# Sigmoid attention and gated FFN on one core: two loads ahead of the unit matrix, the first transposes in half banks, FFN chunk 0 one unit earlier

## The chip, the core and the metric

The kernel runs on one core of one Trainium2 chip. The time is device microseconds (us) of one execution, launch to end. Five engines work side by side, each in its own program order: TensorE (PE, matrix products and transposes; PEld is its loading of weights), VectorE (DVE), ScalarE (ACT), GpSimd (POOL) and SyncE (SP). Three of them issue DMA transfers: SP and ACT through hardware queues, POOL through a software queue that can also convert float32 to float16 on the way. PE writes its results to PSUM, eight banks of 2 KB in each of 128 partitions; DVE and ACT read them from there.

## The reference

Inputs `q`, `k` and `v` have 8 batches, 12 heads, 448 positions and 64 dimensions, in float32. For each batch and head

```python
scores = scale * np.matmul(q, k.transpose(0, 1, 3, 2)) - np.log(S)   # S = 448, scale = 1/8
attn   = 1.0 / (1.0 + np.exp(-scores))                               # sigmoid, no row sums
out    = np.matmul(attn, v)
```

The heads are then put side by side (3584 rows of 768), and a gated feed-forward layer follows, with `w_gate` and `w_val` of 768x1536 and `w_out` of 1536x768:

```python
gate = np.maximum(x @ w_gate, 0.0)
val  = x @ w_val
y    = gate * val @ w_out
```

## The kernel before

**Layout.** The 448 positions of a batch are seven chunks of 64. Six pairs of heads are handled in three groups (`NG = 3`) of four heads. Everything that PE multiplies is float16. Scores are built transposed (keys on the partitions), so that the sigmoid's output can go straight into the product with `v`.

**What has to happen first.** For a group, the keys and queries must be transposed on PE: a transpose is a matmul against a unit matrix (`ident`, built on POOL by `make_identity`, two instructions). `transposed(b, g, ti, c0, c1)` (L199) takes one PSUM bank, transposes chunks c0 to c1 of keys (ti 0) or queries (ti 1) into it, two matmuls a chunk, and returns a function that copies the bank to `qkT` on DVE (L212). `pe_transposes` calls both at once.

**The first loads.** The first four chunks of keys and queries of group 0 come as float32 through the queues of SP and ACT (L126) and are converted to float16, keys on DVE (L679) and queries on ACT (L680). All other loads come through POOL's queue (`load`, L110; `load_v`, L114 and L116; `load_gv`, L148) in the order in which they are written: the remaining keys of group 0, keys and queries of groups 1 and 2, the rest of the queries of group 0, `v`, then the gate and value weights in slices `load_gv(f0, f1)`. Before the first of them POOL builds the unit matrix.

**Batch 0.** Batch 0 is not done like the others, since PE and ACT have to start before much has been loaded. Six slots (`FirstSlot`, L271) run in order: groups 0, 1, 2 with query chunks 0 to 3 (slots 0 to 2), then groups 0, 1, 2 with query chunks 4 to 6 (slots 3 to 5). A slot has four units: unit u multiplies key chunks 2u and 2u+1 with the slot's queries (L240: eight matmuls, four in the last unit) into a pair of PSUM banks, and ACT takes the sigmoid of it (L188). There are two such pairs (`pairp`, `bufs=2`), handed out in turn. So unit n may write only when the sigmoid of unit n-2 has been taken.

**The order by hand.** Instructions stand as the program writes them (`manual_schedule`), no planner moves them. The dictionary `after` says what PE does behind unit u of slot i: transposes, `slots[j].pv` (the product with `v`, L258, and its copy to `xT` on DVE, L185), `ffn_mix(1)`, which takes the next FFN chunk off a queue (`gv`, L312: six gate and six value matmuls, L317, and DVE or ACT work), or `keep_warm` (L172), matmuls on zeros whose result nobody reads, called fillers below. The four other PSUM banks (`bank`) are handed out in turn to transposes, fillers, `pv` and FFN chunks. Around the change the order is: transposes of the second half of the queries behind unit (3, 2); chunk 0 behind (3, 3); chunk 1 and then `pv` of slot 3 behind (4, 1); chunk 2 behind (4, 3). An FFN chunk of the first half needs `pv` of slots 0, 1 and 2, and its two slices of the weights. Chunks 0 and 1 use the first slices, `load_gv(0, 2)`; chunk 2 the next, `load_gv(2, 4)`.

Batches 1 to 7 then follow with units of whole 448 queries, FFN work in between, and the products of the FFN by a scheme with fewer multiplications (L401); the change does not touch these.

Of the kernel before, what the change touches and what calls it, by code (L numbers as in the profile page):

```python
# [17 lines left out]
def kernel(  # L18
# [10 lines left out]
    nc = tc.nc  # L29

    B, H, S, D = q.shape
# [8 lines left out]
    QCUT = 4  # L40
# [35 lines left out]
    def bank(name, shape=(P, 512), dtype=FP32):  # L76
        pool, tag = free[0]
        free.rotate(-1)
        return pool.tile(list(shape), dtype, tag=tag, name=name)

    def bank16(name):
        return bank(name, (P, 1024), FP16)
# [11 lines left out]
    def tiles_of(b):  # L94
        if b not in in_tiles:
            pool = early if b == 1 else inp
            in_tiles[b] = tuple(
                p.tile([P, NPAIR, NCH * D], FP16, tag=t, name=t)
                for p, t in ((pool, "k16"), (pool, "q16"), (vinp, "v16"))
            )  # L100
        return in_tiles[b]

    def rows_of(src, b):
        return src[b].rearrange("(x r) (t c) d -> (r t) x (c d)", r=2, c=NCH)

    def load(b, g0, g1, which, c0=0, c1=NCH):
        for nm, t16, src in zip("kq", tiles_of(b), (k, q)):
            if nm in which:
                xs, cs = slice(2 * g0, 2 * g1), slice(c0 * D, c1 * D)
                nc.gpsimd.dma_start(t16[:, xs, cs], rows_of(src, b)[:, xs, cs])  # L110
# [10 lines left out]
    KCUT = 4  # L121
    first32 = []
# [4 lines left out]
        first32.append(t32)  # L127
    zeros = early.tile([P, S], FP16, name="zeros")
    nc.vector.memset(zeros[:], 0.0)
    ident = early.tile([P, P], FP16, name="ident")  # L130
    make_identity(nc, ident[:])
    load(0, 0, 1, "k", KCUT)
    gate = const.tile([P, 2], FP16, name="gate")
    for g in range(1, NG):
        load(0, g, g + 1, "k")
        load(0, g, g + 1, "q", 0, QCUT)
    load(0, 0, 1, "q", QCUT)
    load_v(0)
# [30 lines left out]
    xT_tiles = {}  # L169
    hT_tiles = {}  # L170

    def keep_warm(count, parts=1):  # L172
        ps = bank("warm_ps")
        n = S // parts
        for _ in range(count * parts):
            nc.tensor.matmul(ps[:, 0:n], zeros[:, 0:P], zeros[:, 0:n], start=True, stop=True)  # L176

    def put_xT(b, pr, q0, qn, src):
# [12 lines left out]
    def qkT_of(b, g):  # L191
        if (b, g) not in qkT_tiles:
            qkT_tiles[(b, g)] = qkTp.tile([P, TW, P], FP16, tag="qkT", name="qkT")
        return qkT_tiles[(b, g)]

    def pe_transposes(b, g, ti, c0=0, c1=NCH):
        transposed(b, g, ti, c0, c1)()

    def transposed(b, g, ti, c0, c1):  # L199
        t16 = in_tiles[b][ti]  # L200
        qkT = qkT_of(b, g)
        trt = bank16("trt")
        for c in range(c0, c1):
            for h in range(2):
                nc.tensor.transpose(  # L205
                    trt[64 * h : 64 * h + 64, c * P : (c + 1) * P],
                    t16[:, 2 * g + h, c * D : (c + 1) * D],
                    ident[:],
                )

        def copy(a0=c0, a1=c1):
            nc.vector.tensor_copy(  # L212
                qkT[:, ti * NCH + a0 : ti * NCH + a1, :].rearrange("p c x -> p (c x)"),
                trt[:, a0 * P : a1 * P],
            )

        return copy
# [449 lines left out]
    def ffn_mix(count, hooks=()):  # L667
        hooks = list(hooks)
        for left in range(count, -1, -1):
            while hooks and hooks[0][0] >= left:  # L670
                hooks.pop(0)[1]()
            if left:
                gv_queue.popleft()()


    nc.scalar.activation(gate[:], zeros[:, 0:2], AF.Sigmoid, bias=sig_bias, scale=qk_scale)
    keep_warm(10, 2)
    k16, q16, _ = in_tiles[0]
    nc.vector.tensor_copy(k16[:, 0:2, 0 : KCUT * D], first32[0])  # L679
    nc.scalar.copy(q16[:, 0:2, 0 : QCUT * D], first32[1])  # L680
    pe_transposes(0, 0, 0, 0, KCUT)
    pe_transposes(0, 0, 1, 0, QCUT)
    keep_warm(2, 2)
    slots = [FirstSlot(half * NG + g, g, half) for half in range(2) for g in range(NG)]
    push_first(0, range(0, 4), False)
    def second_queries():
        for g in range(1, NG):
            pe_transposes(0, g, 1, QCUT, NCH)

    def first_of_second_group():  # L690
        pe_transposes(0, 1, 0, 0, KCUT)
        pe_transposes(0, 1, 1, 0, QCUT)
# [8 lines left out]
        keys(0, 3)  # L701
        keys(3, NCH)

    def ffn_then_pv(i):
        ffn_mix(1)
        slots[i].pv()


    after = {
        (0, 0): lambda: pe_transposes(0, 0, 0, KCUT, NCH),  # L710
        (0, 1): lambda: keep_warm(2, 2),
        (0, 2): first_of_second_group,
        (0, 3): lambda: pe_transposes(0, 1, 0, KCUT, NCH),
        (1, 0): lambda: keep_warm(2, 2),
        (1, 1): lambda: pe_transposes(0, 2, 0),
        (1, 2): lambda: pe_transposes(0, 2, 1, 0, QCUT),
        (1, 3): lambda: keep_warm(2),
# [3 lines left out]
        (2, 3): slots[1].pv,  # L721
        (3, 1): slots[2].pv,
        (3, 2): second_queries,
        (3, 3): lambda: ffn_mix(1),
        (4, 1): lambda: ffn_then_pv(3),
        (4, 3): lambda: ffn_mix(1),
        (5, 1): lambda: pv_then_ffn(4),
        (5, 3): first_of_second_batch,
# [78 lines left out]
    for b in range(1, B):  # L807
# [10 lines left out]
        count = len(bursts)  # L818
# [115 lines left out]
```

## Time and profile before

| | |
|---|---|
| median of 3 runs | 392.06 us (391.92 to 392.45) |
| the profiled execution | 392.07 us |
| its span, first to last instruction | 390.3 us |
| PE busy | 384.5 us, 99% of the span |
| ACT busy | 228.0 us, 58% |
| DVE busy | 283.0 us, 73% |
| POOL busy | 50.8 us, 13% |
| first filler on PE starts | 1.16 us |
| first sigmoid on ACT starts | 7.05 us |

The 1.8 us between the span and the execution's time lie before the first and behind the last instruction. Times in the profile count from the span's start. A busy PE is not PE at its peak: matmuls overlap, and their ends are modelled. In the chain of waits each piece is the work, or the wait, that the next piece had to have; a change of time that does not show on this chain does not show in the total. In a timeline, consecutive instructions of one kind are merged into a line: start, length of the merged stretch, and how many they are.

### The profile page before, as it was taken

Reading aid. Unit: us, or ns where it says so; the run is one execution under the profiler, and the core shown is the slowest. Engines: PE = TensorE matmul, PEld = TensorE weight load, DVE = VectorE, ACT = ScalarE, POOL = GpSimd, SP = SyncE. Lnnn points to the kernel's source line nnn. Section 1 sums busy time; section 2 is a strip of 40 time slices with the busy share of each in tenths; the row PEclk is TensorE's granted clock in tenths of the full one; section 3 lists DMA queues with packets and bytes.
Section 4 is the critical chain, followed back from the end, with each engine's and each line's share of the span. In section 5 each row is a group of like instructions: output and inputs, shape, how many; then the busy total and the mean of one; then the engine's idle time right before and its main releaser. Section 6 shows DMA issues by size and latency. Waiting matters only on the chain.

```text
span 390.3 us, 8791 instructions
## 1 busy us (share of the span) xinstructions
PE 384.5 (99%) x3504; PEld 217.9 (56%) x3504; DVE 283.0 (73%) x557; ACT 228.0 (58%) x482; POOL 50.8 (13%) x75
## 2 busy tenths in 40 slices
PE   8999999999999999999999999999999999999995
PEld 6678776445455545454555554545455555555663
DVE  2453444367387789999758789999987788999563
ACT  4957886784877755555547774545467354333322
POOL 8643404300310300003000300000000000000000
PEclk9999999999999999999999999999999999999999
DMA  9999996997998990226946695132003220000335
GB/s 149 199 199 204 204 203 116 205 204 123 193 187 165 154 236 15 49 47 70 186 94 122 130 206 96 28 66 41 10 22 72 73 79 2 0 3 0 80 89 156
DMA packets 68985, 43.69 MB, mean 112 GB/s; under 512 B 35920, under 2 KB 65616, under 8 KB 68944
## 3 DMA queue, kind: packets, MB, share of 16 engines
q0 software_dynamic: 30768, 23.34, 39.6%
q1 hardware_dynamic: 37664, 19.24, 23.8%
q10 hardware_dynamic: 512, 0.56, 0.5%
q8 instruction: 27, 0.44, 0.4%
q14 instruction: 14, 0.11, 0.1%
HBM read 47.19 MB, written 11.01 MB: 149 GB/s over the span
## 4 chain that ended last, share of the span: by engine, by line
PE 95%; ACT 3%; DVE 1%; issue 0%; DVEq 0%; ACTq 0%
PE u L401 33%; PE g L401 16%; PE y L401 11%; PE qk_ps L240 9%; PE g_ps L317 8%; PE pv_ps L258 8%; PE v_ps L317 7%; ACT PT L188 3%; PE ya L362 1%; PE warm_ps L176 1%; PE trt L205 1%; PE yb L362 1%; DVE ysb L471 0%; DVE S L392 0%; DVE hT L392 0%
## 5 line engine op out<-in xcount | busy, mean ns | idle before, releaser
L188 ACT ACTIVATE PT<-qk_ps 128x448 f16<-128x448 f32 (+3 forms) x318 | 150.9, 585 | 75.2 <-PE qk_ps L240 74.9
L401 PEld LDWEIGHTS <-S 128*128 128x128 f16 x558 | 54.6, 98 | 44.7
L613 DVE TENSOR_TENSOR gsb<-g,gsb 128x448 f32<-128x448 f32 x72 | 42.9, 625 | 10.3 <-PE g L401 10.0
L240 PE MATMUL qk_ps<-qkT 64*64 64x448 f16 (+2 forms) x756 | 47.8, 336 | 0.6 <-ACT PT L188 0.3
L401 PEld LDWEIGHTS <-hT 128*128 128x128 f16 x306 | 28.7, 98 | 22.2 <-issue 4.8
L335 DVE TENSOR_TENSOR hT<-gate_sb,v_ps 128x256 f16<-128x256 f32 (+2 forms) x36 | 16.4, 465 | 33.5 <-PE v_ps L317 16.2
L609 ACT COPY gsb<-u 128x448 f32<-128x448 f32 x48 | 25.6, 558 | 24.0 <-PE u L401 22.9
L453 ACT ACTIVATE ysb<-u 128x384 f32<-128x384 f32 x31 | 15.2, 491 | 38.2 <-PE u L401 33.8
L258 PE MATMUL pv_ps<-PT,v 64*64 64x448 f16 (+2 forms) x756 | 36.9, 329 | 0.0
L185 DVE TENSOR_SCALAR xT<-pv_ps 128x448 f16<-128x448 f32 (+2 forms) x53 | 27.9, 566 | 11.1 <-PE pv_ps L258 10.0
L317 PE MATMUL g_ps<-xT,wg 128*128 128x256 f16 (+2 forms) x216 | 33.5, 291 | 0.0
L317 PE MATMUL v_ps<-xT,wv 128*128 128x256 f16 (+2 forms) x216 | 33.3, 290 | 0.0
L401 PEld LDWEIGHTS <-wg 128*128 128x128 f16 x216 | 20.2, 98 | 21.8 <-issue 4.3
L401 PEld LDWEIGHTS <-wv 128*128 128x128 f16 x216 | 21.1, 98 | 19.7
L240 PEld LDWEIGHTS <-qkT 64*64 64x64 f16 x756 | 18.3, 105 | 21.3 <-issue 14.8
L471 DVE SCALAR_TENSOR_TENSOR ysb<-y,ysb 128x384 f32<-128x384 f32 x29 | 16.1, 556 | 17.9 <-PE y L401 10.4
L258 PEld LDWEIGHTS <-v 64*64 64x64 f16 x756 | 22.0, 107 | 10.5 <-issue 0.7
L110 POOL DMA_DIRECT2D k<-in_k_dram x15 | 11.5, 770 | 109.5 <-DVE rel L223 104.2
L401 PE MATMUL u<-T,hT 128*128 128x384 f16 x132 | 25.1, 326 | 0.0
L317 PEld LDWEIGHTS <-wg 128*128 128x128 f16 x216 | 18.8, 98 | 10.7 <-issue 4.4
L317 PEld LDWEIGHTS <-wv 128*128 128x128 f16 x216 | 20.1, 98 | 7.5
L401 PE MATMUL u<-xT,wg 128*128 128x448 f16 x108 | 23.5, 354 | 0.0
(76 smaller groups left out, 535.5 us busy)
## 6 DMA issues: line engine op xcount, KB each, us to landing
out_dram<-ysb SPq DMA_DIRECT2D x52, 192.0 KB, 2.9
v<-in_v_dram POOLq DMA_DIRECT2D x8, 336.0 KB, 14.8
v<-in_v_dram POOLq DMA_DIRECT2D x16, 168.0 KB, 14.8
k<-in_k_dram POOLq DMA_DIRECT2D x4, 672.0 KB, 11.9
q<-in_q_dram POOLq DMA_DIRECT2D x4, 672.0 KB, 15.3
k<-in_k_dram POOLq DMA_DIRECT2D x9, 224.0 KB, 12.2
q<-in_q_dram POOLq DMA_DIRECT2D x7, 224.0 KB, 12.3
wo<-in_moe_w_out_dram POOLq DMA_DIRECT2D x1, 1536.0 KB, 11.9
```

Of the source, the lines that this page charges most:

```text
L110: nc.gpsimd.dma_start(t16[:, xs, cs], rows_of(src, b)[:, xs, cs])
L185: nc.vector.tensor_scalar(out=xT, in0=src, scalar1=XSCALE, scalar2=None, op0=AOP.mult)
L188: nc.scalar.activation(PT_ap, ps_ap, AF.Sigmoid, bias=sig_bias, scale=qk_scale)
L240: nc.tensor.matmul(out_of(hh)[o : o + 64, :], qkT[rows, c, cols], qkT[rows, NCH + c0 : NCH + c1, cols], start=True, stop=True, tile_positi ...
L258: nc.tensor.matmul(ps[hh][64 * r : 64 * r + 64, 0:qn], v16[rows, 2 * g + hh, c * D : (c + 1) * D], pieces[c][rows, hh, :], start=(c == 0), ...
L317: nc.tensor.matmul(ps[-1][:, 0:qn], wt[:, dc, f * P : (f + 1) * P], xT_tiles[b][:, dc, q0 : q0 + qn], start=(dc == 0), stop=(dc == NDC - 1),)
L335: nc.vector.tensor_tensor(out=hT_tiles[g][:, f, o : o + qn], in0=gate_sb[:, 0:qn], in1=ps[1][:, 0:qn], op=AOP.mult,)
L401: nc.tensor.matmul(ps[:, 0:n], A[:, k_, :], W[:, k_, :], start=(first and k_ == 0), stop=(k_ == kn - 1), skip_group_check=True,)
L453: nc.scalar.activation(o, ps[:, 0:HM], AF.Copy, scale=OUT_SCALE)
L471: nc.vector.scalar_tensor_tensor(out=o, in0=ps[:, 0:HM], scalar=OUT_SCALE, in1=o, op0=AOP.mult, op1=AOP.add)
L609: by(gs[u][i][:], ps[u][:, 0:S])
L613: nc.vector.tensor_tensor(out=gs[u][i][:], in0=ps[u][:, 0:S], in1=gs[u][i][:], op=AOP.add)
```

## The change

On POOL, two loads that stood behind the unit matrix now stand ahead of it: the last three key chunks of group 0 and all keys of group 1. The loads behind them stay in their order.

On PE, the 20 fillers of 224 columns at the start become 22 of 194, and the four fillers between the first transposes and the first unit become two. The first keys and queries (four chunks each) are transposed into four banks of two chunks instead of two banks of four chunks, and copied by four DVE copies of 256 columns instead of two of 512. The copy of key chunks 2 and 3 is the last of the four. The conversion of the first queries is divided: ACT has the first two chunks, DVE the other two. The four fillers behind units (0, 1) and (1, 0) are written in another way, but are the same four matmuls.

FFN chunk 0 moves from behind unit (3, 3) to ahead of it, right behind the transposes; chunk 1 moves from behind unit (4, 1) to ahead of it; `pv` of slot 3 stays behind (4, 1), and chunk 2 behind (4, 3).

```diff
+    load(0, 0, 1, "k", KCUT)
+    load(0, 1, 2, "k")
     ident = early.tile([P, P], FP16, name="ident")
     make_identity(nc, ident[:])
-    load(0, 0, 1, "k", KCUT)
     gate = const.tile([P, 2], FP16, name="gate")
     for g in range(1, NG):
-        load(0, g, g + 1, "k")
+        if g > 1:
+            load(0, g, g + 1, "k")
         load(0, g, g + 1, "q", 0, QCUT)
...
-    def keep_warm(count, parts=1):
+    def keep_warm(count, n=S):
         ps = bank("warm_ps")
-        n = S // parts
-        for _ in range(count * parts):
+        for _ in range(count):
             nc.tensor.matmul(ps[:, 0:n], zeros[:, 0:P], zeros[:, 0:n], start=True, stop=True)
...
-    keep_warm(10, 2)
+    keep_warm(22, 194)
     k16, q16, _ = in_tiles[0]
     nc.vector.tensor_copy(k16[:, 0:2, 0 : KCUT * D], first32[0])
-    nc.scalar.copy(q16[:, 0:2, 0 : QCUT * D], first32[1])
-    pe_transposes(0, 0, 0, 0, KCUT)
-    pe_transposes(0, 0, 1, 0, QCUT)
-    keep_warm(2, 2)
+    half = QCUT // 2 * D
+    nc.scalar.copy(q16[:, 0:2, 0:half], first32[1][:, :, 0:half])
+    nc.vector.tensor_copy(q16[:, 0:2, half : QCUT * D], first32[1][:, :, half:])
+    transposed(0, 0, 0, 0, 2)()
+    other_keys = transposed(0, 0, 0, 2, KCUT)
+    transposed(0, 0, 1, 0, 2)()
+    transposed(0, 0, 1, 2, QCUT)()
+    other_keys()
+    keep_warm(2, S // 2)
...
     def second_queries():
         for g in range(1, NG):
             pe_transposes(0, g, 1, QCUT, NCH)
+        ffn_mix(1)
...
-    def ffn_then_pv(i):
-        ffn_mix(1)
-        slots[i].pv()
...
         (3, 2): second_queries,
-        (3, 3): lambda: ffn_mix(1),
-        (4, 1): lambda: ffn_then_pv(3),
+        (4, 0): lambda: ffn_mix(1),
+        (4, 1): slots[3].pv,
         (4, 3): lambda: ffn_mix(1),
```

More of the change, by code (lines that the diff above doesn't have):

```diff
@@ L702, in first_of_second_batch @@
         keys(3, NCH)
-    def ffn_then_pv(i):
-        ffn_mix(1)
-        slots[i].pv()
     after = {
         (0, 0): lambda: pe_transposes(0, 0, 0, KCUT, NCH),
-        (0, 1): lambda: keep_warm(2, 2),
+        (0, 1): lambda: keep_warm(4, S // 2),
         (0, 2): first_of_second_group,
         (0, 3): lambda: pe_transposes(0, 1, 0, KCUT, NCH),
-        (1, 0): lambda: keep_warm(2, 2),
+        (1, 0): lambda: keep_warm(4, S // 2),
         (1, 1): lambda: pe_transposes(0, 2, 0),
```

## The prediction

> **What bounds the kernel now.** I read the page's busy shares first, then the chain of waits, then the timeline where the change is made.
>
> ```profile
> PE 384.5 (99%) x3504; PEld 217.9 (56%) x3504; DVE 283.0 (73%) x557; ACT 228.0 (58%) x482; POOL 50.8 (13%) x75
> ...
> PE 95%; ACT 3%; DVE 1%; issue 0%; DVEq 0%; ACTq 0%
> ```
>
> PE is the bound of the whole; ACT holds 3% of the chain. The chain of waits of the first 40 us shows where:
>
> ```profile
> 1.16 3.92 PE warm_ps L176 x20
> 5.08 0.99 PE trt L205 x15
> ...
> 7.05 3.35 ACT PT L188 x4
> ```
>
> So the first 7 us are a run-up (first keys, transposes, copies, first scores), 7.05 to 17.14 is bound by ACT, and from 17.18 on every piece is PE's. A microsecond saved before 7.05, or one lost by PE after 17.18, shows in full at the end. The run-up in the timeline:
>
> ```profile
> 4.42 0.43 DVE L679 CAST k<-ysb 128x512 f16<-128x512 f32 x1 [3.32 <-DMA ysb<-in_k_dram]
> 4.71 0.62 ACT L680 CAST q<-ysb 128x512 f16<-128x512 f32 x1 [1.94 <-DMA ysb<-in_q_dram]
> 5.01 0.64 PE L205 MATMUL trt<-ident,k 128*64 128x128 f16 x8
> 5.43 0.64 PE L205 MATMUL trt<-ident,q 128*64 128x128 f16 x8
> 5.69 0.85 DVE L212 COPY qkT<-trt 128x512 f16<-128x512 f16 x2 [0.84 <-PE trt L205]
> 6.00 0.56 PE L176 MATMUL warm_ps<-zeros 128*128 128x224 f16 x4
> ```
>
> The 20 fillers start 0.187 us apart (3.92 less the last one's 0.39, over 19), the four at 6.00 only 0.096 apart (0.56 less 0.26, over 3): PE's clock doubles in between. The transposes still go at the slow rate, two every 0.106 us (four such steps from 5.01 to 5.43), while those at 6.93 need 0.053. The trace's clock record has the full clock from 5.94. And the place of the moved chunks:
>
> ```profile
> 18.85 0.28 PE L240 MATMUL qk_ps<-qkT 64*64 64x192 f16 x4
> 19.06 0.83 PE L317 MATMUL g_ps<-xT,wg 128*128 128x256 f16 x6
> ...
> 20.47 0.53 PE L240 MATMUL qk_ps<-qkT 64*64 64x192 f16 x16
> 20.93 0.83 PE L317 MATMUL g_ps<-xT,wg 128*128 128x256 f16 x6
> 20.95 1.51 ACT L188 ACTIVATE PT<-qk_ps 128x768 f16<-128x768 f32 x2 [1.16 <-PE qk_ps L240]
> ...
> 22.34 0.77 PE L258 MATMUL pv_ps<-PT,v 64*64 64x192 f16 x28
> ```
>
> PE never stands here. ACT takes units (4, 0) and (4, 1) 0.48 us behind their start on PE, while PE works on chunk 1.
>
> **The change, part by part.** The sum is made against the profiled execution: 392.07 us, of which 390.3 are the span and 1.77 lie around it. It is within 0.01 of the median (392.06).
>
> *Fillers and the first transposes.* 22 fillers of 194 columns at the slow rate take 22 x 0.187 x 194/224 = 3.56 us for 3.73, so the last ends 0.17 earlier. Before, the transposes could start 0.32 us behind the last filler's start at 4.68, which is 5.00. Now they wait for the key conversion, 4.42 + 0.43 = 4.85, plus some 0.05 for the signal (the pause between a copy's end, 6.54, and the scores that wait for it, 6.59): 4.90. Gain 0.10.
>
> *Half banks.* Two copies of 512 columns in a row (0.85) become four of 256. Copies of 512 and 384 take 0.423 and 0.354 in the profile, so 256 take 0.285 by the same slope, an estimate. From 4.90 the transposes go through four banks, four matmuls (0.21) each: first keys 4.90, other keys 5.11, first queries 5.32, other queries 5.53. Each bank is ready 0.42 + 0.05 behind its start (0.106 to its last pair, that pair's 0.31, the signal). DVE copies the first keys at 5.37, the first queries at 5.79 to 6.07, the other queries at 6.07 to 6.36. The first unit needs these three only, so it starts at 6.41 for 6.59. The other keys' copy, 6.36 to 6.64, is needed by the transposes behind the unit, at 6.75. The halved conversions are hidden: on ACT 256 columns are some 0.41 (between 0.62 for 512 and 0.20 for the 2 columns of the gate), so 4.71 to 5.12, used at 5.32; DVE's half lies at 4.85 to 5.14, used at 5.53. If that cover went, each late 0.1 would be a late 0.1 of the first unit. Two fillers for four: they end near 6.1, ahead of 6.41, so this is worth nothing as long as the clock rises at 5.94; their removal is cover only for a late clock. Sum of the run-up: -0.19. ACT's stretch starts 0.19 earlier and PE follows it at 17.18.
>
> *The loads on POOL.* The two loads start at 0.74 instead of 1.44 (behind them the unit matrix ends near 3.0, used at 4.90); from the third load on, at 3.02, POOL's queue stands as before. SP and ACT issue nothing new. What it does to the first keys and queries no row shows directly. Bounds: in the DMA view from 1.80 to 3.69 us and then to 4.30
>
> ```profile
> q1 hardware_dynamic: 259, 0.26, 57.6%
> q10 hardware_dynamic: 173, 0.18, 26.3%
> ```
> ```profile
> q0 software_dynamic: 150, 0.06, 78.8%
> q10 hardware_dynamic: 99, 0.09, 40.6%
> ```
>
> POOL's queue (q0) moves nothing until 3.70, although its first load was issued at 1.44. Later in the trace, on an idle queue, a load issued at 63.87 has its first packet 1.46 us later and one at 220.43 after 2.19. So the first was due at 2.9 to 3.6, and waited until the hardware queues were done on each DMA engine. If it waits again, the cost is nothing. If it is served in turn instead from 3.0 on, when some 118 packets of keys and 230 of queries were still to come (7 and 14 on each of 16 engines, at 0.05 us a packet in between), keys land up to 0.38 and queries up to 0.71 later. Working the steps above through from there, the first unit starts at 6.84: +0.25 in place of -0.19. I take nothing, because that is what the row of this very moment shows, and keep +0.44 as the other end. The Trainium skill's page "DMA: Bandwidth & Descriptors", section "Queues, rings and completion order", says that a DMA engine serves its queues in turn, a whole packet of descriptors at a time. By it the sum would take the upper end; the trace, where q0 had nothing before 3.70, does not agree so far. The later landings can only move forward or stay; the closest one, the value weights of chunk 2, lands at 23.93, and PE starts on them at 23.97.
>
> *Chunk 0 and chunk 1.* No work is added; the order decides. Rows: a chunk with the change to scores behind it is 1.41 (19.06 to 20.47); score matmuls up to the next FFN chunk 0.21 for 4, 0.35 for 12, 0.46 for 16; 8 of them up to a `pv` 0.18; a `pv` up to the next scores 0.60. On the old clock, without the gain of the run-up: chunk 0 at 18.85 (its weights land at 16.1 and 19.15, used from 19.4), units (3, 3) and (4, 0) at 20.26, chunk 1 at 20.62, unit (4, 1) at 22.03, `pv` at 22.21, unit (4, 2) at 22.81 and (4, 3) at 22.98. That is 0.13 ahead of the 23.11 of before, since one change between scores and FFN has gone. But (4, 3) writes the pair of banks that ACT reads for (4, 1). ACT now starts on that at 22.03 + 0.48 = 22.51 and needs 0.81 (half of 1.51 and a little, its two overlap): 23.32, with the signal 23.37. Before, this sigmoid ended at 22.46 and nobody waited. Behind the waiting matmul on PE stands chunk 2, and all that follows. So PE loses 0.39 and has 0.13 back: +0.25. Between 0 (if ACT were not later) and +0.35.
>
> *Sum.* 392.07 - 0.19 + 0.25 = 392.13, forecast 392.1: no change that can be measured (0.2%, or 0.78 us, is about what a measurement of this kernel can tell).
>
> **The rivals.**
>
> *The new wait doesn't form, the rest holds.* For it: ACT's lag is read from a merged line. Against it: the same lag of 0.47 to 0.48 stands at (5, 0). Then -0.19 - 0.13: 391.75.
>
> *The early loads hold up the first keys and queries.* As above: 392.07 + 0.25 + 0.25 = 392.6.
>
> *The clock rises later (slower).* This is the one that ends on the other side. The full clock came at 5.94, 4.8 us behind the first filler. The change takes away 0.17 us of early fillers and two later ones, so PE stands more before 5.94. If that is too little work for the rise, PE goes on at half speed. A slot of four units holds, at the full clock, about 0.75 us of score matmuls (seven chunks at 0.107), 0.75 of transposes (14 pairs at 0.053), 0.4 of fillers (four at 0.096) and eight changes of shape at about 0.09: 2.6 of ACT's 3.35. At half speed that is near 4.8, so PE becomes the bound and loses some 0.4 us for every microsecond. Two more slow microseconds decide: 0.8. Up to 4.8 more (as long as it took the first time) give +1.9. The Trainium skill's page "TensorE: Matmul & The Clock Gate", Part 1, has a free-running window of 3413 ns that must be busy; one more window would be 3.4 us, so an estimate of +1.4 us. Against this rival: 3.56 us of unbroken fillers remain, and PE's stretch from 2.5 to 5.9 loses only some 0.2. I take the middle of the 0.8 and the 1.9, +1.35: 393.5.
>
> *Late clock in most runs of before (faster).* If the rise usually came behind 6.75, the four fillers cost 0.75 and the change saves 0.37 more; with no new wait, 392.07 - 0.32 - 0.37 = 391.4, and somewhat below if the transposes gain too. The runs lie between 391.92 and 392.45, which leaves little room for it.
>
> **How the numbers follow.** Forecast 0.45 (391.8 to 392.4), no new wait 0.19, held-up loads 0.16, late clock 0.14, late clock before 0.06. Faster by over 0.2% needs 391.3 or less: 0.06, the last case and its tail. Slower needs 392.85 or more: the late clock and a little of the held-up loads, 0.16. The rest is 0.78. The range runs from 391.4 to 392.9: the three middle cases with their bounds, leaving out the late clock and the lower tail.
>
> **What would show it.** First transposes at 4.90 and first unit near 6.4, first sigmoid near 6.86: run-up right. Conversion of the keys starting later than 4.45: loads held up. Filler spacing of 0.19 behind the transposes, or transposes at 0.106 behind unit (0, 0): late clock. An idle PE of about 0.4 us before the last four score matmuls of slot 4, released by ACT: the new wait. A total outside 391.4 to 392.9 means a mechanism that I did not see, or the late clock.

## The result and the profile after

The changed kernel takes 392.74 us (median of 22 runs, 392.12 to 394.02), the kernel before 392.17 (median of 22 runs beside it, 391.91 to 393.07). The ratio, which rests on all runs and not on the medians alone, is 1.0018, with an interval of 1.0011 to 1.0025. So the changed kernel is slower by some 0.18%: the interval excludes no change at all, but the loss is inside the 0.2% that I count as no change. The 22 runs fall into two groups with nothing between: twelve from 392.12 to 392.75 (their middle is 392.39) and ten from 393.39 to 394.02 (393.58). I call the second one the upper group; the kernel before has one run in 22 above 393.0. The median of 392.74 is thus the top edge of the lower group and stands for neither. The lower group lies 0.22 above the kernel before; the larger part of the loss is the upper group. Two executions of the kernel before, beside the last runs below, took 844.33 and 2242.19 us and are left out of all counts. The profiled execution of the changed kernel is the fastest of the lower group, 392.12 us with a span of 390.3, so its profile shows what becomes of the run-up's gain, but not the upper group.

The page's busy shares and the shares of the chain have hardly moved (PE had 384.5 us and 95% of the chain, and the chain had no DMA in it):

```profile
PE 383.9 (98%) x3504; PEld 217.8 (56%) x3504; DVE 283.2 (73%) x560; ACT 227.8 (58%) x482; POOL 50.7 (13%) x75
...
PE 93%; ACT 3%; DVE 1%; DMA 1%; issue 0%; ACTq 0%; DVEq 0%
```

The chain of waits of the changed kernel up to 24 us (start, length, what) shows both halves of the change:

```profile
0.74 3.73 DMA ysb<-in_k_dram
...
4.50 0.55 DVE k L680
...
5.10 0.32 PE trt L206 x4
...
5.44 0.72 DVE qkT L213 x3
...
6.21 0.44 PE qk_ps L241 x8
...
6.67 3.35 ACT PT L189 x4
...
18.54 0.76 PE g_ps L318 x6
19.30 0.78 PE v_ps L318 x6
...
21.87 0.32 PE qk_ps L241 x8
...
22.27 0.82 ACT PT L189
...
23.13 0.28 PE qk_ps L241 x4
23.41 0.76 PE g_ps L318 x6
```

The first scores start at 6.21 (before: 6.59) and the first sigmoid at 6.67 (before: 7.05), a lead of 0.38. Chunk 0 starts 0.6 earlier. But ACT is on the chain again at 22.27, where it was not before, and chunk 2 starts at 23.34 by the timeline, 0.04 later than before (23.30). From there on the two profiles run side by side, 0.02 to 0.04 apart. The timeline names both losses. Its columns are start, length, engine and line, what and how many, and in brackets the idle time ahead and what ended it. First the kernel before, where units (4, 2) and (4, 3) run in one stretch:

```profile
19.73 0.82 PE L317 MATMUL v_ps<-xT,wv 128*128 128x256 f16 x6
...
22.95 0.42 PE L240 MATMUL qk_ps<-qkT 64*64 64x192 f16 x12
...
23.30 0.83 PE L317 MATMUL g_ps<-xT,wg 128*128 128x256 f16 x6
```

Then the changed kernel:

```profile
18.47 0.83 PE L318 MATMUL g_ps<-xT,wg 128*128 128x256 f16 x6
...
19.25 0.55 PEld L318 LDWEIGHTS <-wv 128*128 128x128 f16 x6 [0.23 <-DMA wv<-in_moe_w_val_dram]
...
22.27 1.93 ACT L189 ACTIVATE PT<-qk_ps 128x768 f16<-128x768 f32 x3 [0.68 <-PE qk_ps L241]
...
22.57 0.34 PE L241 MATMUL qk_ps<-qkT 64*64 64x192 f16 x8
...
23.13 0.28 PE L241 MATMUL qk_ps<-qkT 64*64 64x192 f16 x4 [0.23 <-ACT PT L189]
...
23.34 0.83 PE L318 MATMUL g_ps<-xT,wg 128*128 128x256 f16 x6
```

First loss: the value products of chunk 0 start 0.78 behind its gate products, not 0.67 as before (19.73 less 19.06), because the value weights land only at 19.21. That is 0.11. Second loss: unit (4, 3) starts at 23.13. Unit (4, 2) starts at 22.57, and in the kernel before the unit behind it follows 0.16 later (22.95 in the timeline, 23.11 in the chain), so without a wait it would have been 22.73. PE lost 0.40, waiting for the sigmoid of (4, 1), 22.27 to 23.09. Reckoned in this way, the loss is 0.40 or 0.41 in all seven profiles that have chunk 1 ahead of (4, 1), this one and six of those below (e1, e2, e6, e7, e9, e12), and 0.01 or less in the seven others.

Two questions are left: is the reorder really what eats the run-up's gain, and what makes the upper group?

### The profile page after: what moved, and what is told of

Same layout as the page of the kernel before. It is cut to its first block, busy times and chain, and to the rows that moved or that the text cites. A ratio compares the mean times of both kernels' runs of the same rounds, so it can differ in the third digit from the quotient of the medians.

```text
span 390.3 us, 8795 instructions
## 1 busy us (share of the span) xinstructions
PE 383.9 (98%) x3504; PEld 217.8 (56%) x3504; DVE 283.2 (73%) x560; ACT 227.8 (58%) x482; POOL 50.7 (13%) x75
## 3 DMA queue, kind: packets, MB, share of 16 engines
q0 software_dynamic: 30768, 23.34, 39.6%
## 4 chain that ended last, share of the span: by engine, by line
PE 93%; ACT 3%; DVE 1%; DMA 1%; issue 0%; ACTq 0%; DVEq 0%
PE u L402 33%; PE g L402 16%; PE y L402 11%; PE qk_ps L241 9%; PE g_ps L318 8%; PE pv_ps L259 7%; PE v_ps L318 7%; ACT PT L189 3%; PE ya L363 1%; DMA ysb<-in_k_dram 1%; PE trt L206 1%; PE yb L363 1%; DVE ysb L472 0%; DVE qkT L213 0%; DVE S L393 0%
## 5 line engine op out<-in xcount | busy, mean ns | idle before, releaser
L472 DVE SCALAR_TENSOR_TENSOR ysb<-y,ysb 128x384 f32<-128x384 f32 x29 | 16.1, 556 | 17.9 <-PE y L402 10.4
```

The lines of the kernel that those rows point to most:

```text
L472: nc.vector.scalar_tensor_tensor(out=o, in0=ps[:, 0:HM], scalar=OUT_SCALE, in1=o, op0=AOP.mult, op1=AOP.add)
```

## The experiments

Three theories of the upper group, as the expectations name them. A: fewer fillers make PE's clock rise late in some runs. B: the early loads shift the later ones, and some data comes late. C: the moved chunks meet weights that come late in some runs. In the tables "to chunk 2" is the time from the first scores to the first gate matmul of chunk 2 in the profiled execution: the run-up cancels out of it. Before: 23.30 - 6.59 = 16.71. Changed: 23.34 - 6.21 = 17.13. It grows when PE waits in between.

### Fillers (theory A)

Two kernels give fillers back to the changed one, the third takes them from the kernel before. e1, four late fillers instead of two:

```diff
-    keep_warm(2, S // 2)
+    keep_warm(4, S // 2)
```

> The changed kernel with four fillers instead of two between the first transposes and the first unit; all else as changed. Theory A (the clock): the runs of the changed kernel fall into a group around 392.4 and one around 393.6, and the upper one has the clock rising later, because too little work is left before it. If the late fillers are what is missing, the upper group is gone or is at most 2 runs in 10, and the median is about 392.4. Theory B (the early loads hold up the first keys in some runs): the upper group stays at 4 to 5 runs in 10. Theory C (the moved chunks meet late weights in some runs): it stays too.

e2, 20 early fillers of 224 columns as before:

```diff
-    keep_warm(22, 194)
+    keep_warm(20, S // 2)
```

> The changed kernel with 20 fillers of 224 columns at the start instead of 22 of 194 (0.17 us more of them); two late fillers as changed. Theory A: if the early fillers are what is missing, the upper group is gone; if the late ones are, it stays at 3 to 5 runs in 10, a little fewer than before, as 0.17 us are a small part of what the clock looks back on. The lower group is 0 to 0.1 us slower. Theories B and C: upper group unchanged, 4 to 5 in 10.

e3, the kernel before with the changed kernel's filler columns, 22 of 194 and two late ones:

```diff
-    keep_warm(10, 2)
+    ps = bank("warm_ps")
+    for _ in range(22):
+        nc.tensor.matmul(ps[:, 0:194], zeros[:, 0:P], zeros[:, 0:194], start=True, stop=True)
...
-    keep_warm(2, 2)
+    keep_warm(1, 2)
```

> The kernel before with the two filler edits alone: 22 fillers of 194 columns at the start, two late ones. Order, loads, banks and copies as before. Theory A: the upper group appears here, some 1.2 us above the rest, in 2 to 5 runs of 10. Theories B and C: no such group, all runs within 391.9 to 392.6, 0 to 0.1 us faster than before.

| | median (range), us | ratio to before | at 393.0 or above |
|---|---|---|---|
| e1 | 392.91 (392.41 to 393.87) | 1.0017 [1.0007, 1.0027] | 5 of 12 |
| e2 | 392.65 (392.31 to 393.60) | 1.0009 [1.0000, 1.0017] | 3 of 11 |
| e3 | 392.18 (391.65 to 392.84) | 0.9996 [0.9988, 1.0005] | none of 11 |

Theory A falls. With late fillers back, e1 still has the upper group, and so has e7 below, which has all the fillers of before (5 of 11); with the fillers gone, the kernel before does not get it (e3). And in the profiles the moment of the rise does not follow the fillers: 4.57 in the changed kernel, 6.98 in e1, which has more of them, 4.45 in e2, 7.12 in e3.

The profiled execution of e1 happens to lie in the upper group, at 393.82 us, the only one that does. Its chain of waits goes through POOL's transfers:

```profile
9.80 10.93 DMA wv<-in_moe_w_val_dram
20.73 0.05 issue
20.78 0.83 PE v_ps L318 x6
...
23.80 0.82 ACT PT L189
...
24.66 0.28 PE qk_ps L241 x4
```

and its timeline has PE waiting earlier, too:

```profile
15.44 0.30 PE L259 MATMUL pv_ps<-PT,v 64*64 64x256 f16 x3
...
16.08 0.68 PEld L259 LDWEIGHTS <-v 64*64 64x64 f16 x25 [0.61 <-DMA v<-in_v_dram]
```

The trace has 16 completion signals for each load, which I take as one from each of the 16 DMA engines; it does not name the engine. In this execution 15 signals for the value weights of chunk 0 had come by 18.86, and the last one at 20.73; for the last third of `v`, 15 by 13.93 and the last at 16.04. In the kernel before the 15th and the last for these value weights are 19.09 and 19.15. So here a late last part cost PE twice: 0.57 at `pv` (0.36 behind the kernel before until then, 0.93 after it; a part was regained later) and 0.32 at chunk 0's value weights (0.99 from gate to value products, for 0.67). To that come the 0.40 at unit (4, 3). This execution is 1.75 longer than the profiled one of the kernel before: 0.36 are a later start of the first scores (6.95), 1.21 arise between them and chunk 2, and 0.18 later.

### The parts taken away and done alone (theories B and C)

e4, the changed kernel with chunks 0 and 1 back where they were:

```diff
-        ffn_mix(1)
...
-        (4, 0): lambda: ffn_mix(1),
-        (4, 1): slots[3].pv,
+        (3, 3): lambda: ffn_mix(1),
+        (4, 1): lambda: (ffn_mix(1), slots[3].pv()),
```

> The changed kernel with chunk 0 back behind unit (3, 3) and chunk 1 back behind (4, 1). The wait of the last scores of slot 4 for the sigmoid of (4, 1) should be gone. By the profile after, that wait and the one for the value weights cost 0.43 us: lower group 0.3 to 0.45 us faster than the changed kernel's, about 392.0. Theories A and B: the upper group stays, 4 to 5 runs in 10, also lower by that. Theory C: the upper group is gone.

e5, the kernel before with the early loads alone:

```diff
+    load(0, 0, 1, "k", KCUT)
+    load(0, 1, 2, "k")
     ident = early.tile([P, P], FP16, name="ident")
     make_identity(nc, ident[:])
-    load(0, 0, 1, "k", KCUT)
```

> The kernel before with one part of the change alone: the two loads stand ahead of the unit matrix on POOL. Theory B (the early loads make the upper group of times, since every later load of POOL's queue is then issued about 0.34 us later or one DMA engine lags): 2 to 5 of 10 runs above 393.0, median 392.3 to 392.5. Theory C (only the moved chunks meet late weights): no run more above 393.0 than the kernel before has, and a median as before, 392.1 to 392.3. By my recorded prediction's own sum the loads cost 0: the same as C.

e6, the changed kernel with the unit matrix ahead of all loads again (e5's diff the other way round):

> The changed kernel with the unit matrix ahead of all loads again; the run-up and the moved chunks stay. Theory B: no upper group, median 392.2 to 392.4 (kernel before + 0.1, the moved chunks' 0.4 less the run-up's 0.2 to 0.3). Theory C: the upper group stays, 2 to 5 of 10 runs above 393.0.

e7, the kernel before with the moved chunks alone:

```diff
     def second_queries():
...
+        ffn_mix(1)
...
-        (3, 3): lambda: ffn_mix(1),
-        (4, 1): lambda: ffn_then_pv(3),
+        (4, 0): lambda: ffn_mix(1),
+        (4, 1): slots[3].pv,
```

> The kernel before with the moved chunks alone. The recorded sum has +0.25 for them, which gives 392.45; the two profiles, whose lead of 0.38 us at the first sigmoid turned into a lag of 0.04 at chunk 2, say +0.4, which gives 392.6. Theory B: one group of times, none above 393.1. Theory C: 2 to 5 of 10 above 393.1, as the value weights of chunk 0 are now met early and sometimes late.

e8, the kernel before with the run-up alone (half banks, the divided conversion, fewer filler columns):

```diff
-    keep_warm(10, 2)
+    keep_warm(22, 194)
...
-    nc.scalar.copy(q16[:, 0:2, 0 : QCUT * D], first32[1])
-    pe_transposes(0, 0, 0, 0, KCUT)
-    pe_transposes(0, 0, 1, 0, QCUT)
-    keep_warm(2, 2)
+    half = QCUT // 2 * D
+    nc.scalar.copy(q16[:, 0:2, 0:half], first32[1][:, :, 0:half])
+    nc.vector.tensor_copy(q16[:, 0:2, half : QCUT * D], first32[1][:, :, half:])
+    transposed(0, 0, 0, 0, 2)()
+    other_keys = transposed(0, 0, 0, 2, KCUT)
+    transposed(0, 0, 1, 0, 2)()
+    transposed(0, 0, 1, 2, QCUT)()
+    other_keys()
+    keep_warm(2, S // 2)
```

> The kernel before with the run-up alone: half banks, the first copy split, fewer filler columns; the loads and the order of the chunks as before. Recorded sum: -0.19, which gives 392.0; the two profiles' lead at the first sigmoid gives -0.38, which gives 391.8. One group of times under both theories. If the run-up's gain is lost again at chunk 0's weights (they land when they land), 392.2.

| | what is changed | median (range), us | ratio to before | at 393.0 or above | to chunk 2 |
|---|---|---|---|---|---|
| e4 | run-up, loads | 392.33 (391.78 to 393.69) | 1.0008 [0.9997, 1.0020] | 3 of 11 | 17.06 |
| e5 | loads | 392.20 (391.89 to 393.06) | 1.0004 [0.9996, 1.0013] | 2 of 11 | 16.71 |
| e6 | run-up, order | 392.60 (392.12 to 394.18) | 1.0018 [1.0006, 1.0029] | 4 of 12 | 17.01 |
| e7 | order | 392.80 (392.43 to 393.76) | 1.0023 [1.0014, 1.0031] | 5 of 11 | 17.10 |
| e8 | run-up | 392.15 (391.68 to 393.07) | 0.9998 [0.9989, 1.0007] | 1 of 11 | 17.53 |

The kernel before had a median of 392.25 beside e1 to e4, and of 392.19 beside e5 to e8. The three parts add up, as far as these runs can tell. In medians they cost +0.61 alone (order, e7), +0.01 (loads, e5) and -0.04 (run-up, e8), together +0.58; the change as a whole costs 392.74 - 392.17 = +0.57. In means it is +0.77, +0.11 and -0.07, together +0.81, for +0.74. That the medians agree to 0.01 is luck, since the interval of each ratio is some 0.35 us to either side. So **the order accounts for the loss; the two other parts cost nothing that can be measured**. It costs about as much wherever it is added: in medians 0.61 alone, 0.45 on the run-up (e6 less e8), 0.49 on run-up and loads (the changed kernel's 0.57 less e4's 0.08, each against the kernel before beside it). In e7's profile the wait stands by itself, without the rest of the change, in the chain of waits:

```profile
22.48 0.32 PE qk_ps L240 x8
...
22.88 0.82 ACT PT L188
...
23.75 0.28 PE qk_ps L240 x4
```

On theory B: e5 has no upper group to speak of (its highest runs are 393.01 and 393.06), and e6, without the early loads, has one (393.39 to 394.18). So the early loads are not needed for it, and they cost nothing that can be measured. e4 speaks against theory C: without the moved chunks the upper group should be gone, but 3 of its 11 runs are above 393.0, the highest at 393.69.

The run-up is the surprise. In e8's profile the first scores start at 6.09, 0.50 ahead of the kernel before, and all of that is lost again by chunk 0 (19.06, as before); chunk 1 starts 0.33 late. The chain of waits:

```profile
9.80 10.20 DMA wv<-in_moe_w_val_dram
20.00 0.05 issue
20.05 0.83 PE v_ps L316 x6
```

The chain here is POOL's transfers, not PE. In this execution PE also waits for the last third of `v` (landed at 15.10):

```profile
15.15 0.95 PE L257 MATMUL pv_ps<-PT,v 64*64 64x256 f16 x25 [0.27 <-DMA v<-in_v_dram]
```

e4 shows the same in a faster execution (391.78): a lead of 0.62 at the first scores and still at `pv` of slot 2, 0.43 at chunk 0, 0.26 at chunk 1. The last 0.15 are chunk 0's value weights, which land at 19.41, so that the value products start 0.82 behind the gate products. The rest reached the end in this execution: 0.27 at chunk 2 and 0.29 in its time. In the median of e4's runs nothing of it is seen.

### Which chunk, and the weights by themselves

e9 loads the first two slices of the weights one after the other, so that chunk 0 need not wait for chunk 1's share. On the changed kernel:

```diff
-    load_gv(0, 2, (0,))
+    load_gv(0, 1)
     load(0, 1, NG, "q", QCUT)
-    load_gv(0, 2, (1,))
+    load_gv(1, 2)
```

> The changed kernel with the first two slices of the weights loaded one after the other, so that chunk 0's value weights land near 16.5 us (an estimate: 14.4 for v, then half of the 1.8 and of the 1.95 that the two double slices took) and not at 19.2, and chunk 1's near 19.2. Theory C (the upper group of times is the moved chunk 0 waiting for value weights that one DMA engine brings late): no upper group, median 392.4, since the wait for the value weights of 0.12 goes too and unit (4,3)'s wait of 0.4 stays. Theory B (the early loads): as the changed kernel, 392.7, with 3 to 5 of 10 runs above 393.3.

e10, the same edit on e8 (run-up alone):

> The run-up alone (loads and order as in the kernel before) with the same split of the weight loads. Theory C: the run-up's gain, which the late value weights took back in its profile (lead 0.49 at the first scores, lag 0.33 behind chunk 0), now reaches the end: 391.8, which would beat both kernels. If the gain is lost elsewhere (to the last third of v, for one), 392.15 as without the split.

e11, the kernel before with chunk 0 alone moved ahead of unit (3, 3), and e12, with chunk 1 alone moved ahead of unit (4, 1):

```diff
     def second_queries():
...
+        ffn_mix(1)
...
-        (3, 3): lambda: ffn_mix(1),
```

> The kernel before with chunk 0 alone moved ahead of unit (3,3); chunk 1 stays behind (4,1). If the moved chunks' cost is unit (4,3) waiting for the sigmoid of (4,1), it is not paid here: -0.13 for one change of shape less, 392.1. If it is chunk 0 meeting its value weights early, 392.3 to 392.8, with an upper group.

```diff
-        (4, 1): lambda: ffn_then_pv(3),
+        (4, 0): lambda: ffn_mix(1),
+        (4, 1): slots[3].pv,
```

> The kernel before with chunk 1 alone moved, from behind unit (4,1) to ahead of it; chunk 0 stays behind (3,3). If the cost is unit (4,3) waiting for the sigmoid of (4,1): +0.38 (its scores at 23.07 without a wait, 23.44 with it), 392.55, one group of times. If it is the value weights of chunk 0: as the kernel before, 392.2.

| | median (range), us | ratio to before | at 393.0 or above | to chunk 2 |
|---|---|---|---|---|
| e9 | 393.08 (392.05 to 393.42) | 1.0014 [1.0005, 1.0023] | 6 of 11 | 17.25 |
| e10 | 392.21 (391.87 to 392.72) | 1.0001 [0.9992, 1.0010] | none of 11 | 16.94 |
| e11 | 392.85 (392.57 to 393.76) | 1.0018 [1.0009, 1.0027] | 3 of 11 | 17.50 |
| e12 | 392.53 (392.17 to 393.19) | 1.0010 [1.0001, 1.0019] | 1 of 11 | 17.13 |

e12 came out as the wait of unit (4, 3) has it: 392.53 against 392.17 beside it, and 0.42 more to chunk 2 where I had 0.38. Its chain:

```profile
22.04 0.32 PE qk_ps L240 x8
...
22.44 0.82 ACT PT L188
...
23.30 0.28 PE qk_ps L240 x4
23.58 0.76 PE g_ps L317 x6
```

e11 was a miss for the first half of its expectation, a gain of 0.13, if the wait of (4, 3) were the only cost: it lost 0.79 to chunk 2. The second half, 392.3 to 392.8 if chunk 0 meets its value weights early, came near the median (392.85), but the weights are only a part of it. Chunk 0 ahead of (3, 3) puts three units in a row behind it, (3, 3), (4, 0) and (4, 1). There are two pairs of banks, so the third unit waits for the sigmoid of the first, which ACT could start only when chunk 0 was done. And chunk 0 stood 0.5 us earlier (18.57) and waited for its value weights, which landed at 19.41. The chain, and the row of the waiting unit:

```profile
10.07 9.34 DMA wv<-in_moe_w_val_dram
...
20.61 0.50 ACT PT L188
...
21.15 0.36 PE qk_ps L240 x8
```
```profile
21.15 0.36 PE L240 MATMUL qk_ps<-qkT 64*64 64x192 f16 x8 [0.49 <-ACT PT L188]
```

So each of the two moves, made alone, makes a wait for ACT of the same kind. In the order of before, at most two units stand between two pieces of other work until ACT can follow; the changed order puts (4, 1), (4, 2) and (4, 3) behind chunk 1 with only a `pv` (0.6) among them.

e9 fails for theory C in its simple form. Chunk 0's value weights now land at 17.00, 2.5 us ahead of their use (gate to value products: 0.66, no wait), and the upper group is still there, if lower, 393.08 to 393.42. So late value weights of chunk 0 are not all of it. The edit is not a clean one, though: it also brings the second half of the queries 0.8 us later, to 18.03, and they are used at 18.4.

e10 shows where the run-up's gain went when chunk 0 no longer waited. In its profile a lead of 0.28 at the first scores is 0.04 at the first sigmoid, as the clock rose only at 6.93, and 0.05 at the first gate product of chunk 2; then

```profile
14.63 9.57 DMA wv<-in_moe_w_val_dram
24.20 0.05 issue
24.25 0.83 PE v_ps L316 x6
```

chunk 2's value weights, which land at 24.20, are late, and it goes on 0.28 behind. (In the kernel before they land at 23.93, and PE starts on them at 23.97.)

**What stays open.** The upper group belongs to the new order more than to anything else: 33 of the 79 runs of the kernels with both chunks moved (the changed kernel, e1, e2, e6, e7, e9) are at 393.0 or above, 6 of 55 with the order of before and other parts changed (e3, e4, e5, e8, e10), 4 of 123 of the kernel before. A part of that is only the order's own 0.4, which lifts runs over this bound; the gap in the changed kernel's runs is not. In means the changed kernel loses 0.74, and some 0.56 of that is the ten runs of the group being 1.2 above the other twelve. One execution of the group has a profile, e1's, and there two late loads, a late start and the wait at (4, 3) make up most of the 1.75. That every run of the group is of this kind is not shown; e9 speaks against the weights of chunk 0 as the only place, and e4 against the new order as a condition. So the wait at (4, 3) is shown, and that the order brings the upper group with it is likely by the counts; by what mechanism stays open.

No version beats both kernels: e3, e4, e5, e8 and e10 cannot be told from the kernel before.

## Why the prediction was right, and where it was not

I forecast 392.1, no change that can be measured, in a range of 391.4 to 392.9. The median is 392.74, inside the range but 0.6 above the forecast, near the bound of "slower". That it is inside is partly luck: the median sits on the edge between the two groups of runs, no rival had an upper group, and with one more of the 22 runs in that group the median would have been about 393.1. The sum of -0.19 and +0.25 should have been about 0 and +0.4 to +0.6.

- **The new wait: right in place and size, and the term still too small.** "PE loses 0.39 and has 0.13 back: +0.25". PE lost 0.40 at unit (4, 3), released by ACT, as announced. The step that failed is the one on the weights: chunk 0's weights "land at 16.1 and 19.15, used from 19.4". That time of use was reckoned on the old clock. With the run-up's lead it came to 19.14 (18.47 and the 0.67 of before), and the weights to 19.21: a wait of 0.11, which I had at nothing. With 0.09 had back the term is 0.42 in the profile of the changed kernel, 0.39 in e7's (16.71 to 17.10), above my upper bound of 0.35. In medians it is 0.45 to 0.61, since the runs of the upper group weigh in.
- **The run-up: right up to the first scores, worth nothing that can be measured at the end.** The half-size copies took 0.28 to 0.29 for my 0.285, ACT's half conversion 0.41. Transposes started at 5.10 and not at 4.90, as the keys landed at 4.47 and DVE's conversion took 0.54 in place of 0.43. The first scores came 0.38 earlier, not 0.18; but that is one execution. The first scores start between 6.30 and 6.86 in the five profiles with whole banks and the old fillers (mean 6.56), and between 5.97 and 6.53 in the six with half banks and the new fillers (mean 6.24), so 0.32. PE followed ACT as forecast (16.80 for 17.18 in the changed kernel). The failed step is the premise that a microsecond saved before 7.05 "shows in full at the end": I did not ask what is late next. In the profiles it is POOL's stream: the last third of `v` (e8), the value weights of chunk 0 (the changed kernel, e4, e8), the weights of chunk 2 (e10). From the row of the last one, landing at 23.93 for a start at 23.97, I read only that an earlier load does no harm, not that an earlier PE may gain nothing. But this slack of 0.04 belongs to one execution. In that profile 15 of the load's 16 signals had come by 23.14, and with the old order and run-up the same load had a slack of 0.47 in e5 (23.58 to 24.05) and 0.73 in e3 (23.37 to 24.10). What no single row shows is the spread: the value weights of chunk 0 landed between 18.97 and 20.73 in the twelve profiles that load them as before.
- **The loads on POOL: right sum, wrong steps.** e5 gives +0.01. But the two loads did not start at 0.74, and from the third load on POOL's issues did not stand as before. POOL in the changed kernel:

```profile
1.25 1.58 POOL L110 DMA_DIRECT2D k<-in_k_dram  x2 [0.80 <-POOLq L921]
...
2.82 0.23 POOL masks.py:197 MEMSET ident<- 128x128 f16 x1
...
3.12 0.29 POOL masks.py:199 TENSOR_SCALAR_AFFINE_SELECT ident<-ident 128x128 f16<-128x128 f16 x1
...
3.36 0.71 POOL L110 DMA_DIRECT2D q<-in_q_dram  x1
```

The unit matrix used to begin at 0.74, the first load at 1.44. In none of the six profiles with the early loads did POOL's first load start before 1.24, so the unit matrix had stood mostly in time that was lost anyway. The gain is 0.19 for two loads, the price some 0.34 for the nine that follow (3.36 for 3.02, and so on); from the value weights of chunk 0 on, issued at 9.81 in both, it is gone. "The later landings can only move forward or stay" was wrong in its ground, though the landings that matter did not show it (19.21 for 19.15, 23.66 for 23.93).

- **The rival of held-up first loads: did not happen.** In the DMA view from 1.80 to 3.69 POOL's queue (q0) has six packets, with loads issued from 1.25 on:

```profile
q1 hardware_dynamic: 250, 0.25, 67.0%
q10 hardware_dynamic: 145, 0.15, 21.9%
q0 software_dynamic: 6, 0.00, 1.0%
```

Its first packet is at 3.57, and first keys land at 4.47 for 4.40. Over all profiles they land between 4.28 and 4.47 in the six with the early loads and between 4.25 and 4.58 in the eight others, so they were not held up. (At 3.0 the trace has 134 packets of keys and 244 of queries still to start, not 118 and 230, so the price would have been a little higher.) Why POOL's queue came so late is not shown. Its first packet comes as the hardware queues run out (their last packets start at 4.02 and 4.32), but the trace does not list packets by DMA engine, so a wait "until the hardware queues were done on each DMA engine" cannot be read from it. It is not the time of issue alone: issued at 1.24 or 1.25, the first packet came at 3.56 to 3.66, and issued at 1.43 or 1.44, at 3.55 to 3.84. By the rule of the Trainium skill's page "DMA: Bandwidth & Descriptors", section "Queues, rings and completion order" (each DMA engine goes round its queues, a packet at a time), a queue with work should have been served in between; the traces show no packet of it before 3.55, so either the rule does not hold here or the queue had nothing ready until then.

- **The rival of the late clock: wrong in its cause, and its price was met by luck.** The rise did not follow the fillers, but it did move: from 3.83 to 7.12 over the 14 profiles. Where it came 0.62 behind the first scores, the first sigmoid had lost 0.23 (e3: 0.09 ahead of the kernel before at the first scores, then 0.14 behind) and 0.24 (e10). That is 0.4 us for every microsecond, as I had it, but not by PE becoming the bound of a slot: the first eight score matmuls took 0.64 in place of 0.41, and from there on ACT kept its 3.36 to 3.37 a slot. No profile has the clock rise so late that it would try the price of a whole slot. What was wrong is that a late rise would be an effect of the change. The Trainium skill's page "TensorE: Matmul & The Clock Gate", Part 1, says that the window of 3413 ns runs freely, so that the moment of the rise is set by where in it the work begins. The trace agrees: the full clock lasts 385.706 or 382.293 us in the profiles, 3.413 apart.

## What to carry to other kernels

Before a lead is counted, go down the chain to the next loads that have to land, and compare the lead with the slack between landing and use. Take the slack from several profiles: here the landing of one load moved by 1.8 us between executions, and a lead of 0.3 could not be counted in full. When work is moved among units that alternate between two buffers, count how many units then stand in a row between two long pieces: the third waits for the consumer of the first. And where an engine's first load does not start at once, what stands ahead of it may be nearly free, and moving it behind the loads makes it cost its full time.

## What the runs showed of the hardware

- The moment at which PE's clock rises is not the kernel's: 3.83 to 7.12 us in 14 profiles, with no order by the amount of filler work. In the five profiles with the old run-up the first scores come in the order of the rise, from 6.30 (rise at 5.12) to 6.86 (6.90), half a microsecond apart, so a run-up can't be judged by one profile. In the six with half banks and the new fillers that order is not seen.
- The last of a load's 16 completion signals can lag behind the other 15. At the value weights of chunk 0 it came 0.07 us behind the 15th in the kernel before, 0.85 in e8 and 1.88 in e1, with the same transfers. In e8 and e1 PE started on them 0.05 behind the last signal, so one part's lag is the load's.
- POOL's first load starts at 1.24 or 1.25 when it stands ahead of the unit matrix (six profiles), although POOL could begin a memset at 0.73 or 0.74 (eight profiles).
- DVE's conversion of the first keys (128x512 from float32) took 0.43 in the eight profiles without the early loads. In the six with them either it was longer (0.54 in the changed kernel, 0.66 in e5, 0.68 in e1), or the load that POOL was issuing from 4.07 on took 0.81 or 0.82 in place of 0.72 (e2, e4, e9, conversion 0.43). What ties the two together was not tried.
